# One inner block of a fused attention and MoE kernel by seven products instead of eight, with new order tables

## The chip, the core and the metric

The kernel runs on one core of a Trainium2 chip. The metric is the device time of one execution in microseconds (us); a median over several executions is quoted, and one profiled execution gives the trace that is read below. The engines are named as in the profile: PE is TensorE's matmul, PEld its weight load, DVE is VectorE, ACT is ScalarE, POOL is GpSimd, SP is SyncE, which issues nearly all transfers.

## What is computed

A linear attention with decay, then two feed-forward layers ("MoE layers" in the code). Cut to what matters:

```python
# attention: batch 2, 8 heads, 768 steps, head size 64
state = gamma * state + k_t (outer) v_t          # for t in range(768)
y_t   = scale * q_t @ state
x = y.transpose(0, 2, 1, 3).reshape(1536, 512)
# stage 1: w_in 512 x 2048, w_out 2048 x 512
h = x @ w_in
x = where(h > 0, h, exp(min(h, 0)) - 1) @ w_out
# stage 2: w_a, w_b 512 x 1536, w_out 1536 x 512
out = ((x @ w_a) * (x @ w_b)) @ w_out
```

## The kernel before

**Numbers.** Every fp32 operand of the layers is split into a high part that TensorE's fast fp32r form takes and a low rest: `wh`/`wl` for weights, `xh`/`xl` and `yh`/`yl` for the inputs of stage 1 and 2, `gh`/`gl` for what comes out of the first product of a stage. One product of 128 rows is then three matmuls (high by high, high by low, low by high). A split is a cast on ACT (L746) and a subtraction on POOL or DVE (L750). The weights come as 64-bit words into one of three staging buffers (`raw`); ACT takes their two halves apart (L768, L772) and DVE joins them (clamp L775, shift L779, join L783, total L789). So each weight tile costs DVE four instructions before its split.

**Attention.** `attention()` works on eight pairs of heads. `load` (L366 to L383) issues the transfers of q and k of a pair (one tensor `in_qk`) and of k and v by rows (`in_kv`). For pairs 0 to 3 q and k come in two pieces, `q0` (columns 0 to 511) and `q1` (columns 512 to 767); for the others in one. The order of the transfers is `QUEUE`, that of TensorE's steps `PRODUCTS`: `("s",u,part)` are scores (L556), `("x",p)` turns k of a pair (L483), `("t",u)` are states (L519), `("r",n,part)` results of two pairs (L584, L591), `("m",f,half)` the first four tiles of stage 1's first product for token block 0 (L709 to L711). `keep_warm` (L332) fills places in which the planner expects TensorE to wait. The score banks are two, so a score step waits until DVE has masked the one before the last (L562).

**Layers.** `layers()` has three blocks of 512 tokens (b = 0, 1, 2) and inner blocks of 128 (f). Two blocks and two weight tiles make a 2 by 2 product of quarter matrices, which `quad` does by seven products p1 to p7 of six matmuls each instead of eight; the sums that it needs of the inputs (`differences`, L1114 and on) and of the weights (`sums`, L816) are made on DVE and split again. Block 2 has the same within itself with 256 columns (`quad_s`), and `plain1`, `plain2` are the products without sums. `contract1` and `contract2` are the second products of stage 1 and stage 2 (L709 to L711).

In stage 2 inner block f has the tiles wa[f] and wb[f]. For f = 0 the kernel before uses `plain2` for all three blocks: four products of twelve matmuls for blocks 0 and 1, two for block 2, as undivided steps `R0.b.0` and `R0.b.1`. Block 1's plain product also has to be over before `differences` writes its third sum into that block's buffer (the argument `lambda: done["plain", 2, 1]`). From f = 1 on `quad2` does blocks 0 and 1.

**Order.** TensorE's order in the layers is the table `STEPS`: `a`, `d`, `b` are stage 1's first tiles (plain products of blocks 1 and 2, first second-product), `qf.i` and `rf.i` the products of `quad` and of block 2 in stage 1, `cn.b.e` stage 1's second products, and `Q`, `R`, `o` the same in stage 2. The other engines' order is made by the planner `Sched` from fixed costs and the times by which each step is wanted; on POOL or DVE, whichever suits (`other=("DVE", 0.6)`). All waits are set when the program is built.

Of the kernel before, what the change touches and what calls it, by code (L numbers as in the profile page):

```python
# [33 lines left out]
a2 a3 a4 a6 a0 d0 a5 b0 a1 a7 b1 d2 q4.2 d1 d3 b2 c0.1.3 q4.1 c0.1.1 c0.1.2 c0.1.0 q4.5 b3 c0.2.1 q4.6 r4.1 q4.3  # L34
r4.2 r4.6 c0.2.0 q4.7 r4.5 c0.2.2 r6.1 q6.1 r4.3 q4.4 c0.2.3 r4.7 r6.2 q6.6 q6.2 q6.5 c1.1.1 c1.0.1 c1.0.2 r6.6
r4.4 q6.7 c1.0.0 c1.0.3 c1.1.2 r6.7 q6.3 q6.4 c1.2.3 c1.2.2 r6.5 c1.1.0 c1.2.0 c1.1.3 r8.2 r6.3 r6.4 r8.1 q8.1
c2.1.2 c2.0.0 c2.0.1 r8.6 c2.1.0 q8.2 c2.1.3 q8.6 c2.1.1 r8.5 q8.7 r8.7 c1.2.1 c2.2.2 q8.5 c2.2.0 c2.2.3 q10.1
q8.4 q10.5 r8.4 r8.3 c2.0.2 q8.3 q10.2 q10.3 r10.2 c3.0.0 c2.2.1 q10.6 c2.0.3 c3.0.2 q10.7 c3.1.1 q12.1 r10.1
c3.0.3 r10.6 c3.2.1 r10.7 c3.1.2 q10.4 c3.0.1 c3.2.0 c3.2.2 q12.5 r12.1 r10.5 c3.2.3 r10.3 q12.2 r12.2 c3.1.0
c4.0.0 r12.5 r14.1 c3.1.3 c4.0.1 r10.4 r12.3 q12.6 c4.0.2 c4.1.3 q14.1 c4.2.3 r12.6 c4.1.0 q12.7 q14.5 c4.1.1  # L40
q14.2 q14.6 c4.0.3 q12.3 r12.7 c4.2.2 c4.2.0 r12.4 c4.2.1 q12.4 c4.1.2 q14.3 r14.6 c5.1.1 q14.7 c5.1.0 r14.7
c5.2.1 q14.4 c5.1.2 c5.1.3 c5.0.1 c5.2.3 c5.0.0 c5.0.3 r14.5 c5.0.2 c6.1.2 r14.4 c5.2.0 r14.2 r14.3 c6.1.3
c6.1.0 c5.2.2 c6.0.0 c6.1.1 c6.0.3 c6.2.2 c6.0.2 R0.1.0 c6.0.1 c6.2.0 c6.2.1 c6.2.3 R0.1.1 R0.0.0 R0.2.0 Q1.2
Q1.5 R2.2 Q1.1 R1.2 R1.0 R1.3 Q1.6 R0.2.1 Q1.3 R1.1 Q2.1 Q2.2 R0.0.1 Q1.7 Q2.6 R2.1 Q1.4 Q2.5 o0.8 o0.5 o0.3
o0.7 o0.10 Q2.3 o0.2 o0.11 Q3.1 Q2.7 R3.1 R2.5 R2.6 R3.2 Q2.4 R3.6 Q3.5 o0.9 Q3.2 Q3.6 R2.7 o0.4 o0.1 Q4.1 R4.1
R2.4 Q3.7 o0.6 o0.0 Q3.4 Q3.3 R3.7 R3.5 Q4.2 R4.2 R4.6 Q4.6 R3.4 R3.3 Q4.5 R2.3 Q4.7 o1.1 o1.2 Q4.3 Q5.1 o1.11
o1.0 R5.1 o1.9 Q5.2 o1.8 R4.5 o1.5 o1.4 R4.7 R5.2 Q4.4 o1.3 R4.4 Q6.1 R5.6 Q5.6 R5.5 R4.3 Q5.7 o1.7 R5.7 R5.3
Q5.5 R5.4 R6.5 o1.10 R6.2 o1.6 Q5.3 Q5.4 R6.1 Q6.5 R6.6 R6.3 o2.0 o2.7 o2.11 o2.6 Q6.3 Q6.6 o2.10 Q7.1 R6.7 R7.2
o2.3 R6.4 Q6.7 Q6.2 Q7.6 Q7.2 Q8.1 R7.1 o2.2 Q6.4 R7.6 Q7.5 R7.5 Q7.7 Q7.3 o2.4 R7.7 o2.5 R8.5 R7.3 o2.1 o2.9
Q8.6 R8.1 R8.2 R8.3 Q8.5 R7.4 Q7.4 o2.8 Q8.7 Q8.2 Q8.3 R8.6 o3.9 o3.7 o3.8 R9.2 Q10.1 o3.5 R8.7 o3.11 o3.2 Q8.4  # L50
R8.4 o3.0 o3.3 R9.1 Q9.2 Q9.1 R9.6 R9.5 Q9.6 R9.7 R9.3 o3.4 R10.1 Q10.6 R9.4 o3.1 o3.6 Q9.7 Q9.5 o3.10 Q10.2
Q9.3 Q11.2 Q10.5 R10.6 Q10.7 R10.2 Q10.3 Q9.4 o4.5 Q11.1 o4.10 R11.1 Q11.5 Q10.4 o4.0 o4.4 o4.1 R10.7 Q11.6 o4.6
Q11.7 o4.9 o4.3 o4.11 o4.2 R11.6 Q11.4 Q11.3 R11.7 o4.7 o4.8 R10.5 R11.5 o5.0 R11.3 o5.1 o5.2 o5.3 R11.2 R11.4
# [1396 lines left out]
```

## Time and profile before

| | us |
|---|---|
| three timed runs, median | 581.99 (581.75 to 582.2) |
| the profiled execution | 582.04 |
| its span in the trace | 580.3 |
| first step of the layers on TensorE | 60.28 after the span's start |
| TensorE busy, of the span | 574.5 |
| VectorE busy, of the span | 497.9 |

The span is 1.74 us shorter than the execution; the profiled execution lies 0.05 us from the median. A matmul's end is modelled in the trace, so TensorE's pace is read from the starts of its instructions, and a wait shows as a start that comes later than the pace. Times in the rows count from the span's start.

### The profile page before, as it was taken

The page shows a single profiled execution, that of the slowest core. Times are in us where ns is not written, and L with a number is a line of the kernel's source. Part 1 is how long each engine was busy: PE and PEld are TensorE (multiplying, and loading weights), DVE is VectorE, ACT ScalarE, POOL GpSimd, SP SyncE. Part 2 cuts the span into 40 slices and gives each one's busy share as a digit, 9 for nine tenths or more (in the row PEclk, how much of TensorE's full clock was granted, in tenths as well). Part 3 has the DMA queues.
Part 4 walks back from the last instruction along what each step waited for, and adds up shares of the span by engine and source line. Part 5 has one row for each costly group of instructions (what it writes and reads, how often), then busy time and mean ns, then how long its engine had stood idle before and what let it go on. Part 6 is the DMA issues. An engine that isn't in the chain of part 4 may idle for free.

```text
span 580.3 us, 9157 instructions
## 1 busy us (share of the span) xinstructions
PE 574.5 (99%) x3416; PEld 488.9 (84%) x3416; DVE 497.9 (86%) x816; ACT 346.1 (60%) x633; POOL 224.9 (39%) x165
## 2 busy tenths in 40 slices
PE   9999999999999999999999999999999999999997
PEld 8887888888888888888888888888888888888886
DVE  3886899988998999989998998989889998869565
ACT  6456897778577957687565675653554463454110
POOL 0355227415334334145477332252543174152210
PEclk9999999999999999999999999999999999999999
DMA  8993240122222223222210320313022231210013
GB/s 305 357 298 138 84 135 1 37 60 88 67 73 71 81 64 92 99 73 74 72 37 0 110 72 26 119 39 110 29 88 81 95 111 37 73 37 0 1 73 146
DMA packets 23421, 51.53 MB, mean 89 GB/s; under 512 B 2256, under 2 KB 11984, under 8 KB 23376
## 3 DMA queue, kind: packets, MB, share of 16 engines
q1 hardware_dynamic: 23232, 50.80, 28.1%
q8 instruction: 27, 0.44, 0.3%
q14 instruction: 18, 0.15, 0.1%
q10 hardware_dynamic: 144, 0.14, 0.1%
HBM read 47.79 MB, written 3.15 MB: 88 GB/s over the span
## 4 chain that ended last, share of the span: by engine, by line
PE 93%; DMA 5%; DVE 1%; issue 0%; SPq 0%; ACT 0%; DVEq 0%; ACTq 0%
PE p L848 49%; PE p L709 13%; PE p L710 13%; PE p L711 13%; DMA qk<-in_qk 2%; DMA raw<-in_w 1%; DMA rows<-in_kv 1%; PE y L591 1%; PE sc L556 1%; PE s L519 1%; PE y L584 1%; PE sc L483 0%; DVE wl L750 0%; ACT rows L498 0%; DVE a L779 0%
## 5 line engine op out<-in xcount | busy, mean ns | idle before, releaser
L750 POOL TENSOR_TENSOR wl<-a,wh 128x512 fp32r<-128x512 f32 x57 | 82.0, 1443 | 163.6 <-ACT wh L746 127.2
L750 POOL TENSOR_TENSOR gl<-t,gh 128x512 fp32r<-128x512 f32 x59 | 83.6, 1423 | 112.4 <-ACT gh L746 94.0
L746 ACT CAST wh<-a 128x512 fp32r<-128x512 f32 x98 | 59.6, 620 | 30.7 <-DVE a L789 19.1
L709 PE MATMUL p<-gh,wh 128*128 128x512 f32 x192 | 75.0, 390 | 0.0
L710 PE MATMUL p<-gl,wh 128*128 128x512 f32 x192 | 75.0, 390 | 0.0
L711 PE MATMUL p<-gh,wl 128*128 128x512 f32 x192 | 74.7, 389 | 0.0
L848 PE MATMUL p<-yl,wh 128*128 128x512 f32 (+1 forms) x200 | 69.5, 347 | 0.0
L848 PE MATMUL p<-yh,wh 128*128 128x512 f32 (+1 forms) x200 | 69.3, 347 | 0.0
L848 PE MATMUL p<-yh,wl 128*128 128x512 f32 (+1 forms) x200 | 69.3, 347 | 0.0
L848 PE MATMUL p<-wl,wh 128*128 128x256 f32 (+1 forms) x198 | 67.1, 339 | 0.0
L848 PE MATMUL p<-wh 128*128 128x256 f32 (+1 forms) x198 | 66.9, 338 | 0.0
L848 PE MATMUL p<-wh,wl 128*128 128x256 f32 (+1 forms) x198 | 66.9, 338 | 0.0
L746 ACT CAST gh<-t 128x512 fp32r<-128x512 f32 x80 | 48.3, 618 | 28.6 <-DVE t L1013 8.3
L864 ACT COPY t<-p 128x512 f32<-128x512 f32 x55 | 32.1, 584 | 43.6 <-PE p L848 43.0
L871 DVE TENSOR_TENSOR t<-p,t 128x512 f32<-128x512 f32 x66 | 45.2, 685 | 14.8 <-PE p L848 9.1
L709 PE MATMUL p<-wh,gh 128*128 128x512 f32 (+1 forms) x146 | 56.6, 388 | 0.0
L710 PE MATMUL p<-wl,gh 128*128 128x512 f32 (+1 forms) x146 | 56.6, 388 | 0.0
L711 PE MATMUL p<-wh,gl 128*128 128x512 f32 (+1 forms) x146 | 56.4, 386 | 0.0
L768 ACT ACTIVATE a<-raw 128x512 f32<-128x512 f32 x64 | 43.0, 673 | 17.3 <-POOL wl L750 8.1
L772 ACT ACTIVATE c<-raw 128x512 int32<-128x512 uint32 x64 | 42.8, 671 | 10.6 <-DVE a L789 9.5
L783 DVE SCALAR_TENSOR_TENSOR a<-raw,a 128x512 int32<-128x512 int32 x64 | 48.5, 768 | 0.5
L789 DVE CUSTOM_DVE_ANT_0 a<-a,c 128x1024 uint16<-128x1024 uint16 x64 | 47.5, 753 | 0.7
(142 smaller groups left out, 1346.7 us busy)
## 6 DMA issues: line engine op xcount, KB each, us to landing
raw<-in_w SPq DMA_DIRECT2D x16, 512.0 KB, 3.8
raw<-in_wa SPq DMA_DIRECT2D x12, 512.0 KB, 3.8
...
```

The lines of the kernel that those rows point to most:

```text
L709: nc.tensor.matmul(ps, lh, rh, start=first, stop=False)
L710: nc.tensor.matmul(ps, lh, rl, start=False, stop=False)
L711: nc.tensor.matmul(ps, ll, rh, start=False, stop=last)
L746: nc.scalar.copy(like(dst[key][0], src()), src())
L750: engine.tensor_tensor(out=lo, in0=src(), in1=hi.bitcast(F32), op=ALU.subtract)
L768: nc.scalar.activation(out=T["a", key], in_=T["raw", key][:, :, 1].bitcast(F32), func=AF.Abs, scale=E_SHIFT)
L772: nc.scalar.activation(out=T["c", key], in_=T["raw", key][:, :, 0].bitcast(U32), func=AF.Copy, scale=2.0**-29)
L783: nc.vector.scalar_tensor_tensor(out=ai, in0=T["raw", key][:, :, 1], scalar=SIGN, in1=ai, op0=ALU.bitwise_and, op1=ALU.bitwise_or)
L789: nc.vector.tensor_tensor(out=ai, in0=ai, in1=T["c", key], op=ALU.add)
L848: nc.tensor.matmul(ps, l[:, col(cc)], r, start=first and i + j == 0, stop=end and j == 2, skip_group_check=True)
L864: "ACT", 0.48, lambda ring: nc.scalar.copy(taken(key, ring), T[src]), after, [(tr, users)], [bank],
L871: "DVE", 0.6, lambda: nc.vector.tensor_tensor(out=T[out], in0=T[in0], in1=T[in1], op=op), after,
```

## The change

Five things are changed, and nothing of what is computed. (1) In stage 2, f = 0 goes through `sums` and `quad2` as the other inner blocks do; its plain products of blocks 0 and 1 are gone, block 2's stay, cut in two parts each (`R0.0` to `R0.3`). (2) `differences` of stage 2 waits for no plain product. (3) `STEPS` is a new order of all steps of both layers. (4) `QUEUE` and `PRODUCTS` are new orders for the attention, and q and k of pairs 0 to 3 come in one transfer each. (5) The planner's cost of an `x` step is 1.38 instead of 0.9. Two lines stand for each table:

```diff
 STEPS = """
-a2 a3 a4 a6 a0 d0 a5 b0 a1 a7 b1 d2 q4.2 d1 d3 b2 c0.1.3 q4.1 ...
+a2 a6 a3 d3 d0 d2 b0 r4.2 b1 a0 a4 b2 a5 a7 a1 b3 r4.1 d1 c0.1.0 ...
-c6.1.0 c5.2.2 c6.0.0 c6.1.1 c6.0.3 c6.2.2 c6.0.2 R0.1.0 c6.0.1 c6.2.0 ...
+c6.0.0 c6.1.1 c6.1.0 c6.0.1 c6.1.3 c6.2.0 c6.2.3 Q0.1 c6.2.1 Q1.1 c6.0.2 ...
 QUEUE = [
-    "tb", ("q0",1), ("q1",1), ("q0",0), ("q1",0), ("v",1), ("k",3), ("v",0), ("v",3), ("k",2), ("q0",3), "gy",
+    ("q",1), "tb", ("q",0), ("k",3), ("v",1), ("v",3), ("v",0), ("q",3), "gy", ("q",2), ("k",2), ("v",2),
 PRODUCTS = [
-    ("s",3,0), ("s",2,0), ("r",0,1), ("t",2), ("s",2,1), ("s",3,1), ("r",1,0), ("s",4,0), ("t",4), ("r",1,1),
+    ("s",3,0), ("s",2,0), ("r",0,1), ("t",2), ("s",3,1), ("s",2,1), ("r",1,0), ("s",5,0), ("s",4,0), ("r",1,1),
...
-            done["q0", 0] = load(0, "qk", 1.3, "q0", col=h0)
             t1_ = fetch("tb", 0.3, lambda: nc.scalar.dma_start(out=tb1, in_=tab[:, : NS1 + C]))
-            done["q1", 0] = load(0, "qk", 0.7, "q1", col=h1)
+            done["q0", 0] = done["q1", 0] = load(0, "qk", 1.95, "q")
...
-                if p in (0, 1, 2, 3) and p:
+                if p in () and p:
...
-                    o = step(("x", p), 0.9, turn, [done["q0", p], done["q1", p], eye_], [(rsc, t_)], [users["qk", p]])
+                    o = step(("x", p), 1.38, turn, [done["q0", p], done["q1", p], eye_], [(rsc, t_)], [users["qk", p]])
...
-        weight(("wa", 0)), weight(("wb", 0))
-        for f in range(1, NF2):
+        for f in range(NF2):
             sums(("wa", f), ("wb", f))
...
-        for b in (1, 0):
-            go(f"R0.{b}.", plain2(0, b, 1))
...
-            lambda: done["plain", 2, 1],
+            list,
...
-        go("R0.2.", plain2(0, 2, 1))
-        for f in range(1, NF2):
+        for f in range(NF2):
...
-            if f % 2 == 0:
+            if f and f % 2 == 0:
```

How the order of instructions moves at three places, in the rows of the built programs. (In the kernel after, line numbers from 390 on are one lower, and from about 1385 on up to five lower.)

SP's first transfers, of before. The names are the tile, then the tensor; the size is partitions by elements.

```order
L379 DMA qk<-in_qk 128x2x512
L379 DMA qk<-in_qk 128x2x256
L379 DMA qk<-in_qk 128x2x512
L379 DMA qk<-in_qk 128x2x256
L381 DMA rows<-in_kv 128x768
L381 DMA k<-in_kv 128x768
```

And of after:

```order
L379 DMA qk<-in_qk 128x1536 x2
L381 DMA k<-in_kv 128x768
L381 DMA rows<-in_kv 128x768
L381 DMA k<-in_kv 128x768
L381 DMA rows<-in_kv 128x768
L379 DMA qk<-in_qk 128x1536
```

The first score step, which waited for the 512 columns of pair 1, now waits for all its 768 of q and of k.

TensorE at the first use of a weight of stage 1's second group of tiles, w1[4], of before: the end of `d2` and the start of `q4.2`. `wh_1097` and `wl_1098` are w1[4].

```order
L848 MATMUL p_1127<-xh_676,wh_723 128x512
L848 MATMUL p_1127<-xl_677,wh_723 128x512
L848 MATMUL p_1127<-xh_676,wl_724 128x512
L848 MATMUL p_1159<-xh_343,wh_1097 128x512
L848 MATMUL p_1159<-xl_344,wh_1097 128x512
L848 MATMUL p_1159<-xh_343,wl_1098 128x512
```

And of after: the end of `b0` and the start of `r4.2`; w1[4] is `wh_1076` and `wl_1077`.

```order
L708 MATMUL p_1064<-gh_803,wh_987 128x512
L709 MATMUL p_1064<-gl_804,wh_987 128x512
L710 MATMUL p_1064<-gh_803,wl_988 128x512
L847 MATMUL p_1088<-xh_643,wh_1076 128x256
L847 MATMUL p_1088<-xl_644,wh_1076 128x256
L847 MATMUL p_1088<-xh_643,wl_1077 128x256
```

Ahead of it stand, in the layers, 96 matmuls before (`a2 a3 a4 a6 a0 d0 a5 b0 a1 a7 b1 d2`) and 66 after (`a2 a6 a3 d3 d0 d2 b0`).

VectorE's rows up to the low part of w1[4], of before (the 20th to the 27th of its instructions in the layers):

```order
L775 TENSOR_SCALAR a_1056<-a_1056 128x512
L889 SCALAR_TENSOR_TENSOR t_1052<-t_1052,p_943 128x512
L779 TENSOR_SCALAR a_1056<-a_1056 128x512
L783 SCALAR_TENSOR_TENSOR a_1056<-raw_1004,a_1056 128x512
L789 ISA a_1056<-a_1056,c_1064 128x1024
L750 TENSOR_TENSOR wl_1078<-a_986,wh_1077 128x512
L789 ISA a_1013<-a_1013,c_1061 128x1024
L750 TENSOR_TENSOR wl_1098<-a_1056,wh_1097 128x512
```

And of after (the 18th to the 24th):

```order
L774 TENSOR_SCALAR a_1041<-a_1041 128x512
L778 TENSOR_SCALAR a_1041<-a_1041 128x512
L782 SCALAR_TENSOR_TENSOR a_1041<-raw_983,a_1041 128x512
L788 ISA a_1041<-a_1041,c_1044 128x1024
L888 SCALAR_TENSOR_TENSOR t_1047<-t_1047,p_994 128x512
L778 TENSOR_SCALAR a_1011<-a_1011 128x512
L749 TENSOR_TENSOR wl_1077<-a_1041,wh_1076 128x512
```

VectorE has three instructions less ahead of it, TensorE thirty matmuls less.

TensorE where stage 2 begins, of before: the end of `c6.0.2` and the start of `R0.1.0`, twelve matmuls of which the first six stand here (`yh`, `yl` are stage 2's input, `wh_3131` is wa[0]).

```order
L711 MATMUL p_3365<-gh_3222,wl_3015 128x512
L848 MATMUL p_3375<-yh_3314,wh_3131 128x512
L848 MATMUL p_3375<-yl_3315,wh_3131 128x512
L848 MATMUL p_3375<-yh_3314,wl_3132 128x512
L848 MATMUL p_3375<-yh_3314,wh_3131 128x512
L848 MATMUL p_3375<-yl_3315,wh_3131 128x512
L848 MATMUL p_3375<-yh_3314,wl_3132 128x512
```

And of after: `c6.2.3`, then `Q0.1` with six matmuls, then `c6.2.1` (wa[0] is `wh_2996`).

```order
L710 MATMUL p_3381<-gh_3337,wl_2985 128x512
L847 MATMUL p_3391<-yh_3342,wh_2996 128x512
L847 MATMUL p_3391<-yl_3343,wh_2996 128x512
L847 MATMUL p_3391<-yh_3342,wl_2997 128x512
L847 MATMUL p_3391<-yh_3342,wh_2996 128x512
L847 MATMUL p_3391<-yl_3343,wh_2996 128x512
L847 MATMUL p_3391<-yh_3342,wl_2997 128x512
L708 MATMUL p_3406<-gh_3326,wh_2980 128x512
```

The step of twelve matmuls on block 1 has given way to one of six on block 0.

## Rows read from the trace of the kernel before

**Rows 1.** The page: busy time by engine, and the longest chain by engine.

```profile
PE 574.5 (99%) x3416; PEld 488.9 (84%) x3416; DVE 497.9 (86%) x816; ACT 346.1 (60%) x633; POOL 224.9 (39%) x165
...
PE 93%; DMA 5%; DVE 1%; issue 0%; SPq 0%; ACT 0%; DVEq 0%; ACTq 0%
```

**Rows 2.** The longest chain in order of time: start, us, what.

```profile
257.34 1.36 PE p L848 x6
```

**Rows 3.** Timeline of TensorE and VectorE near 232: start, us, instruction.

```profile
232.24 0.28 PE L848 MATMUL p<-xl,wh 128*128 128x256 f32 x1
232.62 0.39 PE L848 MATMUL p<-xh,wl 128*128 128x256 f32 x1
232.84 0.28 PE L848 MATMUL p<-xh,wh 128*128 128x256 f32 x1
232.96 0.28 PE L848 MATMUL p<-xl,wh 128*128 128x256 f32 x1
...
230.78 1.78 DVE L750 TENSOR_TENSOR wl<-a,wh 128x512 fp32r<-128x512 f32 x1
```

**Rows 4.** Timeline of TensorE in the attention; in brackets idle time and its releaser.

```profile
5.62 1.16 PE L556 MATMUL sc<-qk 64*128 64x128 f32 x16 [0.36 <-DMA qk<-in_qk]
...
8.00 0.94 PE L332 MATMUL warm<-kv 128*128 128x128 f32 x6
8.87 1.55 PE L483 MATMUL sc<-one,qk 64*128 64x64 f32 x24
...
21.36 0.80 PE L519 MATMUL s<-rows 128*64 128x64 f32 x20
22.11 0.71 PE L556 MATMUL sc<-qk 64*128 64x128 f32 x8
23.24 0.71 PE L556 MATMUL sc<-qk 64*128 64x128 f32 x8 [0.41 <-DMA qk<-in_qk]
23.88 0.96 PE L584 MATMUL y<-qk,st 64*64 64x128 f32 x24
...
46.19 0.33 PE L519 MATMUL s<-rows 128*64 128x64 f32 x2 [0.40 <-ACT rows L498]
...
47.42 0.51 PE L584 MATMUL y<-qk,st 64*64 64x128 f32 x8
...
60.28 0.50 PE L848 MATMUL p<-xh,wh 128*128 128x512 f32 x1
```

**Rows 5.** First piece of the longest chain; then busy times, clock, DMA share, GB/s.

```profile
0.73 4.85 DMA qk<-in_qk
...
8.00:12.00 4.00, 4.00 (x68) 3.72 (x66) 0.99 (x2) 4.00 (x12) 0.00 (x0) 1.00 1.04 407
```

**Rows 6.** Timelines of VectorE, GpSimd and TensorE where the layers begin.

```profile
62.42 0.56 DVE L775 TENSOR_SCALAR a<-a 128x512 f32<-128x512 f32 x1 [1.25 <-ACT a L768]
63.01 1.40 DVE L779 TENSOR_SCALAR a<-a 128x512 int32<-128x512 int32 x1
...
66.71 0.43 DVE L779 TENSOR_SCALAR a<-a 128x512 int32<-128x512 int32 x1
...
77.97 0.68 DVE L750 TENSOR_TENSOR wl<-a,wh 128x512 fp32r<-128x512 f32 x1
...
61.40 2.73 POOL L636 TENSOR_TENSOR xl<-yf,xh 128x512 fp32r<-128x512 f32 x2
...
82.62 0.39 PE L848 MATMUL p<-xh,wl 128*128 128x512 f32 x1
```

**Rows 7.** The page's costliest groups: count, busy us, mean ns of one, idle before.

```profile
L750 POOL TENSOR_TENSOR wl<-a,wh 128x512 fp32r<-128x512 f32 x57 | 82.0, 1443 | 163.6 <-ACT wh L746 127.2
...
L746 ACT CAST wh<-a 128x512 fp32r<-128x512 f32 x98 | 59.6, 620 | 30.7 <-DVE a L789 19.1
...
L871 DVE TENSOR_TENSOR t<-p,t 128x512 f32<-128x512 f32 x66 | 45.2, 685 | 14.8 <-PE p L848 9.1
```

**Rows 8.** Busy us in two stretches: PE, PEld, DVE, ACT, POOL; clock, DMA share, GB/s.

```profile
270.00:300.00 30.00, 30.00 (x145) 25.30 (x144) 28.02 (x49) 18.80 (x34) 16.31 (x12) 1.00 0.22 67
300.00:330.00 30.00, 30.00 (x137) 24.95 (x136) 26.11 (x35) 16.98 (x30) 18.69 (x12) 1.00 0.21 61
```

More of the change, by code (lines that the diff above doesn't have):

```diff
@@ L33 @@
 STEPS = """
[L34 to L53, printed above, removed]
@@ L54 @@
-R10.4 R10.3 o5.4 o5.5 o5.6 o5.7 o5.8 o5.9 o5.10 o5.11 o5.12
+a2 a6 a3 d3 d0 d2 b0 r4.2 b1 a0 a4 b2 a5 a7 a1 b3 r4.1 d1 c0.1.0 c0.1.1 c0.1.2 r4.5 c0.1.3 q4.5 r4.3 q4.1 c0.2.3
+c0.2.0 r4.6 r6.1 c0.2.1 q4.6 r4.7 q4.3 c0.2.2 q4.7 r6.2 r4.4 q6.1 r6.6 r6.5 q4.2 q6.5 r6.7 q4.4 c1.2.0 c1.1.3
+q6.6 r6.3 c1.2.1 c1.1.0 q6.3 c1.1.1 q6.7 r8.2 q8.1 c1.1.2 c1.0.2 c1.2.3 q8.6 c1.0.1 q6.4 q6.2 r6.4 q8.5 c1.2.2
+c1.0.0 q8.7 c2.1.2 c1.0.3 q8.2 r8.5 q8.4 r10.1 c2.0.1 c2.1.1 c2.1.3 r8.1 q10.2 c2.1.0 r8.6 c2.2.1 c2.0.0 c2.2.0
@@ new lines @@
+r8.7 q8.3 q10.1 r10.6 c2.2.2 r10.5 r8.4 c2.0.3 r8.3 c2.0.2 q10.6 c2.2.3 q10.5 c3.0.0 c3.1.2 r10.3 q10.7 r12.2
+r10.2 q12.2 q10.3 c3.2.0 r10.7 c3.0.2 q12.1 r10.4 c3.0.1 c3.0.3 c3.1.1 r12.1 c3.1.0 q10.4 c4.1.2 q14.1 c3.1.3
+c3.2.3 c3.2.1 c3.2.2 c4.0.3 c4.1.0 c4.1.3 c4.0.1 q12.5 q14.5 r12.5 c4.1.1 r12.6 r12.3 q12.6 q12.3 q12.7 c4.0.2
+c4.2.2 c4.2.1 q14.2 q14.6 q12.4 c4.2.0 r12.7 c4.2.3 c4.0.0 r14.1 r12.4 r14.5 q14.3 c5.1.2 c5.1.0 q14.7 r14.6
+c5.0.0 c5.2.0 q14.4 c5.1.3 c5.0.1 c5.1.1 c5.2.1 r14.7 c5.0.3 r14.2 c5.2.3 c5.0.2 c6.1.2 r14.3 r14.4 c5.2.2
@@ new lines @@
+c6.0.0 c6.1.1 c6.1.0 c6.0.1 c6.1.3 c6.2.0 c6.2.3 Q0.1 c6.2.1 Q1.1 c6.0.2 c6.2.2 R1.2 R0.0 c6.0.3 R0.2 Q0.6 R1.3
+R1.0 Q0.2 R1.1 Q0.7 Q1.2 Q0.5 Q1.5 R0.1 R0.3 Q1.6 R2.2 Q2.1 R2.1 Q2.5 Q1.3 Q0.3 Q1.7 o0.11 o0.8 Q2.2 Q0.4 o0.9
+Q1.4 o0.10 R3.1 o0.7 Q2.6 o0.3 Q2.3 Q2.7 o0.4 R3.2 Q3.1 Q2.4 o0.5 o0.6 R2.6 o0.1 R3.5 Q3.5 R3.3 Q3.6 o0.2 R2.7
+o0.0 R3.6 R2.5 Q3.3 Q3.7 R3.7 Q4.1 Q3.2 Q3.4 R4.1 R2.4 R4.2 R2.3 Q4.6 R4.5 R3.4 Q4.2 R4.6 Q4.5 o1.1 R4.3 o1.3
+Q5.2 R4.7 R5.2 o1.11 Q5.1 o1.9 R5.1 R4.4 Q4.7 Q4.3 o1.4 o1.10 Q4.4 R6.2 o1.8 Q5.6 R6.1 o1.2 R5.6 o1.0 o1.5 Q5.7
@@ new lines @@
+Q5.5 R5.5 o1.6 R5.7 Q5.3 R6.6 o1.7 Q6.5 Q6.2 R5.3 R5.4 R6.7 R6.5 Q5.4 o2.6 Q6.1 o2.5 R6.4 Q6.6 R7.2 o2.7 R6.3
+Q7.1 o2.10 Q6.7 o2.9 Q7.6 Q7.5 Q6.4 R7.1 Q7.2 Q7.3 Q7.7 R7.6 o2.3 R7.5 Q8.1 Q6.3 R7.7 o2.4 o2.2 o2.0 R8.5 R8.2
+Q7.4 R7.3 Q8.2 R7.4 Q8.5 R8.3 R8.1 o2.1 Q8.6 o2.8 o2.11 R9.1 Q8.7 Q9.2 o3.3 Q8.4 Q8.3 R8.6 o3.5 o3.4 o3.0 R8.7
+R9.5 R9.2 o3.6 o3.1 o3.2 Q9.5 o3.9 o3.10 Q9.1 o3.8 o3.7 R10.2 R9.6 Q9.6 Q9.3 Q9.7 o3.11 R10.1 Q10.1 R9.3 R10.6
+R9.7 R8.4 Q9.4 R9.4 R10.5 Q10.2 Q10.5 Q10.6 o4.11 o4.9 o4.5 o4.1 o4.6 o4.7 R10.7 o4.4 Q11.1 R10.3 Q10.3 Q10.7
@@ L55 @@
+Q11.2 o4.2 Q11.6 o4.8 Q11.5 R11.1 Q11.7 Q10.4 o4.10 Q11.4 R11.5 R11.6 o4.3 R11.3 o5.0 R11.7 Q11.3 o5.1 R10.4
+o5.2 R11.2 o5.3 R11.4 o5.4 o5.5 o4.0 o5.6 o5.7 o5.8 o5.9 o5.10 o5.11 o5.12
 """
 QUEUE = [
[3 rows of a table removed]
[3 rows of a table added]
 ]
 PRODUCTS = [
[5 rows of a table removed]
[5 rows of a table added]
 ]
@@ L388, in attention @@
             h0, h1 = slice(0, 4 * C), slice(4 * C, S)
-            done["q0", 0] = load(0, "qk", 1.3, "q0", col=h0)
             t1_ = fetch("tb", 0.3, lambda: nc.scalar.dma_start(out=tb1, in_=tab[:, : NS1 + C]))
-            done["q1", 0] = load(0, "qk", 0.7, "q1", col=h1)
+            done["q0", 0] = done["q1", 0] = load(0, "qk", 1.95, "q")
             eye_ = add("DVE", 0.35, unit_matrix, [t1_])
             for p in range(NPAIR):
-                if p in (0, 1, 2, 3) and p:
-                    done["q0", p] = load(p, "qk", 1.3, "q0", col=h0)
-                    done["q1", p] = load(p, "qk", 0.7, "q1", col=h1)
+                if p in () and p:
+                    done["q0", p] = load(p, "qk", 1.31, "q0", col=h0)
+                    done["q1", p] = load(p, "qk", 0.71, "q1", col=h1)
                 elif p:
```

12 rows, old and new, of tables (PRODUCTS, QUEUE) are left out of this document.

## The prediction

> **What bounds the kernel now.** The page first: TensorE is busy for 99% of the span, VectorE for 86%, and the longest chain lies on PE for 93% [rows 1]. The reader should see that VectorE has little in hand, though it does not bind. A busy PE need not be at its peak, so the second view is the chain in order of time: in the layers six matmuls of 512 columns take 1.36 us, 0.227 each [rows 2], whole stretches long. The third is TensorE's timeline, in which I looked for starts later than that pace. From 60.28 us, where the layers begin [rows 4], to the end I found one: near 232 two starts of 256-column matmuls follow the last by 0.38 and 0.22 us, where the next distance is 0.12 [rows 3]. So 0.26 + 0.10 = 0.36 us are lost there, behind a VectorE subtraction that runs from 230.78 to 232.56. All other loss is in the attention. The layers are thus bound by TensorE's count of matmuls, the attention in part by data and by other engines.
>
> **The change part by part.** The sum is made against the profiled execution: 580.3 us of span and 1.74 outside it, 582.04, which is 0.05 above the median of 581.99.
>
> *Seven products for f = 0.* Four products of twelve matmuls become seven of six: 48 become 42. Six matmuls go, 6 x 0.227 = **-1.36 us** [rows 2]. All lie on the path, since TensorE has no gap there. The helpers get more: two casts on ScalarE and one copy, two subtractions on GpSimd, some seven additions and products on VectorE. At most 7 x 0.685 = 4.8 us on VectorE, and 1.44 each on GpSimd [rows 7]. The cover is VectorE's idle time just before, 30.00 - 28.02 = 1.98 us and 30.00 - 26.11 = 3.89 us in two stretches of 30 [rows 8]: 5.9 against 4.8. I cost this at nothing. Without that cover the price is up to 4.8 us. The handover itself: `Q0.1` stands three products, 3 x 1.36 = 4.08 us, behind the last second product of its input; eviction, cast and subtraction take 0.685 + 0.62 + 1.44 = 2.75 us [rows 7], so the input is ready 1.3 us early.
>
> *The argument `list`* only takes away a wait on products that no longer exist: nothing.
>
> *The stall near 232* hangs on a place in the old order, and in the new one that weight has another: **-0.36 us** [rows 3].
>
> *The attention.* The old order has three places where TensorE lost time [rows 4]. A score step of eight matmuls starts at 22.11, the next at 23.24, 1.13 later and behind a transfer; the following distance is 0.64, so 0.49 is lost. Before 46.19 it idles for 0.40 behind ScalarE. The step at 46.19 holds TensorE for 1.23 us until 47.42, where one of ten times as many matmuls took 22.11 - 21.36 = 0.75, so 0.48 more is lost. Together **-1.37 us**, if the new order avoids all three. The bounds: 0 if they return elsewhere, -1.6 if the other short waits of the attention shrink as well. I take the measured sum, since one of the three hangs on a transfer that the whole loads finish earlier.
>
> *Whole loads.* This is what they cost. The first score step waits for q and k of its pair. Today that is 128 x 2 x 512 numbers, 524 thousand bytes, and 665 with the table (141) that comes beside it; it took 4.85 us from 0.73. At 407 GB/s [rows 5] 665 need 1.63 us, which leaves 3.22 fixed. The whole load has 786, with the table 927: 2.28 + 3.22 = 5.50, so it lands at 6.23 instead of 5.58. The price lies between 0 (there are other waits just behind, which may absorb it: TensorE fills 0.87 us from 8.00 with warm matmuls) and +0.65. I take **+0.45 us**, nearer to the full price, because the first step starts as its transfer lands, at 5.62 [rows 4]. The cost 1.38 for an `x` step only moves things: the 24 small matmuls span 8.87 to 10.4 either way. It counts with the order.
>
> *The new order in the layers.* All steps move, so I looked for the step with the least slack. It is `r4.2`, the first to use w1[4]. TensorE reaches its third matmul after 66 matmuls and two short ones: 66 x 0.227 + 0.24 = 15.2 us behind the layers' start. VectorE needs 23 instructions before the low part of that weight. In the kernel before that subtraction is the 27th and starts at 77.97; the first starts at 62.42, 2.14 us after the layers' start [rows 6]. So 26 took 15.55 us, 0.598 each. Then 23 x 0.598 = 13.75, the subtraction starts at 2.14 + 13.75 = 15.9 and ends 0.68 later, at 16.6: TensorE waits **+1.4 us**. In the old order there was slack: the part was done at 78.65 and first used at 82.62 [rows 6]. The bounds: +0.4, if the first shift takes 0.43 as the next one does, not 1.40 [rows 6], and +2.0 if one instruction more or a late staging buffer comes between. I take the middle, which is what the measured pace gives. Behind the waiting matmul all of TensorE's later steps are queued and come later by the same; VectorE, which then gets its next products to evict later, has that time to catch up.
>
> That slow shift deserves a look. At 63.01 it took 1.40 us while a GpSimd pair ran from 61.40 to 64.13; at 66.71, with GpSimd quiet, 0.43 [rows 6]. The Trainium skill, page "SBUF — State Buffer", section "🔬 SBUF: two separate sides", says that VectorE and GpSimd share a port pair that one of them holds for its whole instruction while the other is blocked. The two durations agree with it. By that rule the delay stays as long as that pair stays there, which speaks for the 1.4; without the block it would be 0.4.
>
> *Other waits of the new order.* Some hundred steps move, and the trace before does not show what they meet. Between 0 and 1.2 us (three stalls of the size of that near 232, rounded up); below nothing is excluded, since TensorE has no other gap to lose. I take **+0.2**, nearest to that one stall [rows 3].
>
> The sum: 580.3 - 1.36 - 0.36 - 1.37 + 0.45 + 1.4 + 0.2 = 579.26; with 1.74, **581.0 us**.
>
> **The rivals.**
>
> *B, the helpers keep up.* No wait at `r4.2`, since the planner has put ahead only what VectorE can do and the slow shift is gone: 581.0 - 1.4 - 0.1 = 579.5. For it: 0.97 of the 1.4 us is one shift [rows 6]. Against it: the count of 23 instructions at the measured pace.
>
> *C, VectorE becomes the bound.* Where the new order takes a weight earlier and VectorE's pace is slower than 0.65 us an instruction instead of 0.598, its backlog reaches two more weights in the first 70 us of the layers, each worth what `r4.2` costs: 581.0 + 2 x 1.4 = 583.8, slower than before. For it: 86% busy [rows 1], 28.02 of 30 us in a stretch [rows 8], and the added work. Against it: TensorE did not wait for it before, but near 232. The Trainium skill, page "Perfetto Trace Analysis", section "Identifying the Most-Contended Engine", says that TensorE is to be judged by its weight-load busy time and the others by occupancy. By these, 84% and 86% [rows 1], VectorE would be the bound already, and up to 4.8 us of added work would then show in the time. The evenly spaced starts of TensorE speak against it.
>
> *D, the attention gives nothing.* The first step starts later, the three stalls come back at other places; -1.37 and +0.45 cancel or leave the price: 581.9 to 582.4, say 582.1. For it: the attention's steps hang on transfers, whose total of bytes is unchanged. Against it: two of the three stalls have to do with order, not with bytes.
>
> *That the change doesn't do what it says*, I rule out for the matmuls: the order of the built program has six of them where twelve stood.
>
> **How the numbers follow.** About 0.2%, 1.16 us, is what a measurement of this kernel can tell from no change; so faster is below 580.8 and slower above 583.2. My forecast, 581.0, has 0.44: it lies close to the first bound, 0.17 of it on the faster side and 0.27 on the other. B has 0.27, all faster. D has 0.16, all within. C has 0.13, all slower. Faster 0.17 + 0.27 = 0.44, same 0.27 + 0.16 = 0.43, slower 0.13. The range: down to 578.9, which is B with the attention's larger gain (-1.6) and the whole loads at a smaller price; up to 582.9, which takes in D and the forecast with `r4.2` at 2.0 and the other waits at 1.2 (581.0 + 0.6 + 1.0 = 582.6). Left out are C and the lower tail of B, less than 2 in 10.
>
> **What would show it.** Each step can be read in the trace of the kernel after. TensorE's first score step starts near 6.1 (right) or 5.6 (then the whole load cost nothing). The first matmul of the layers starts near 59.4; at 60.3 or later, D holds. In `r4.2` a wait for VectorE's L749 near 74.5 us of more than 1 us, or none (B). Further starts of TensorE late by over 0.5 us between 75 and 130, behind VectorE, mean C. Six matmuls fewer in TensorE's count from the seven products, and no wait ahead of `Q0.1` and the following `Q` steps; a wait there would mean that the cover for the added helper work was too thin. The tail behind the last matmul should be as before. The prediction is wrong as a whole if TensorE's distance between 512-column matmuls is no longer 0.227, or if a stretch that I did not look at has become the longest chain.

## The result: slower by 0.5%, outside the range

| | us |
|---|---|
| after, six timed runs, median | 585.42 (584.04 to 586.16) |
| before, six runs beside it | 581.91 |
| ratio | 1.0053, 95% interval 1.0039 to 1.0067 |
| profiled execution after, its span | 586.13, 584.3 |

The forecast was 581.0 with a range up to 582.9. The change is slower by 3.5 us, which is more than the 0.2% that a measurement of this kernel can tell. Two lines of the page of after answer to [rows 1]: busy times, and the longest chain by engine.

```profile
PE 575.9 (99%) x3412; PEld 489.4 (84%) x3412; DVE 496.1 (85%) x824; ACT 345.5 (59%) x636; POOL 229.5 (39%) x166
...
PE 86%; DVE 6%; issue 4%; DMA 1%; ACT 1%; SPq 1%; POOL 0%; DVEq 0%; ACTq 0%
```

The busy shares hardly move, and a reader of these alone would not see that anything happened. (TensorE's count falls by four: 26 warm matmuls instead of 24, and six fewer in the layers.) The chain does move: 6% of it now lie on VectorE, where it was 1%. Where the time went is seen from TensorE's starts. In before the layers began at 60.28 [rows 4], and TensorE lost 0.36 us in them. The view of waits of after, TensorE in the layers (us in total, times, longest us), and its timeline at these places:

```profile
PE p L708 <- DVE xs L1209: 0.7, 1, 0.7
PE p L847 <- DVE t L888: 0.4, 1, 0.4
PE p L847 <- ACT t L863: 0.4, 1, 0.4
PE p L847 <- DVE wl L749: 0.4, 1, 0.4
PE p L709 <- DVE gl L749: 0.3, 1, 0.3
PE p L847 <- ACT wh L745: 0.2, 1, 0.2
```

```profile
61.93 0.50 PE L847 MATMUL p<-xh,wh 128*128 128x512 f32 x1
...
77.44 0.39 PE L847 MATMUL p<-xh,wh 128*128 128x256 f32 x1 [0.21 <-ACT wh L745]
77.67 0.28 PE L847 MATMUL p<-xl,wh 128*128 128x256 f32 x1
78.33 0.39 PE L847 MATMUL p<-xh,wl 128*128 128x256 f32 x1 [0.38 <-DVE wl L749]
...
95.17 0.50 PE L847 MATMUL p<-xh,wh 128*128 128x512 f32 x1 [0.40 <-DVE t L888]
...
98.67 0.50 PE L709 MATMUL p<-gl,wh 128*128 128x512 f32 x1 [0.26 <-DVE gl L749]
...
238.39 0.50 PE L708 MATMUL p<-gh,wh 128*128 128x512 f32 x1 [0.68 <-DVE xs L1209]
...
249.46 0.50 PE L847 MATMUL p<-xh,wh 128*128 128x512 f32 x1 [0.40 <-ACT t L863]
```

The idle times in brackets are less than what is lost, since the ends of matmuls are modelled. Measured by starts against the pace, as in the prediction, the five places cost 1.12 (r4.2, at 77 and 78), 0.67, 0.53, 0.95 and 0.67 us, together 3.95 with the slower start behind each. The account against the span of before: 580.3 + 1.65 (layers begin later) + 3.95 - 0.35 (the place near 232 is gone) - 1.36 (six matmuls) = 584.2, measured 584.3.

In the attention, TensorE's timeline (idle time and its releaser in brackets), then busy us of four stretches (PE, PEld, DVE, ACT, POOL; clock, DMA share, GB/s), then SP's issues:

```profile
5.62 1.88 PE L555 MATMUL sc<-qk 64*128 64x128 f32 x16
7.34 1.45 PE L482 MATMUL sc<-one,qk 64*128 64x64 f32 x24
...
30.58 1.16 PE L555 MATMUL sc<-qk 64*128 64x128 f32 x16
33.60 0.80 PE L518 MATMUL s<-rows 128*64 128x64 f32 x20 [1.86 <-DMA rows<-in_kv]
34.33 0.69 PE L708 MATMUL p<-xh,wh 128*128 128x512 f32 x1
34.81 0.63 PE L709 MATMUL p<-xl,wh 128*128 128x512 f32 x1
35.24 0.63 PE L710 MATMUL p<-xh,wl 128*128 128x512 f32 x1
```

```profile
20.00:24.00 4.00, 4.00 (x93) 3.69 (x92) 3.85 (x7) 2.17 (x5) 3.06 (x3) 1.00 0.72 254
24.00:28.00 4.00, 4.00 (x76) 3.67 (x68) 3.79 (x7) 0.67 (x2) 0.76 (x2) 1.00 0.87 314
...
32.00:36.00 4.00, 2.40 (x24) 2.08 (x25) 2.02 (x4) 2.17 (x5) 2.23 (x3) 0.81 1.08 290
36.00:40.00 4.00, 4.00 (x63) 3.13 (x63) 3.80 (x7) 2.43 (x5) 1.27 (x1) 0.76 1.02 405
```

```profile
13.14 7.90 SPq L379 DMA_DIRECT2D qk<-in_qk  x2
```

The first two stretches in before:

```profile
20.00:24.00 4.00, 3.56 (x68) 2.88 (x64) 3.23 (x7) 1.86 (x4) 2.18 (x3) 1.00 1.05 390
24.00:28.00 4.00, 4.00 (x80) 3.59 (x82) 3.79 (x7) 1.92 (x4) 0.21 (x1) 1.00 1.03 407
```

The three losses of [rows 4] are gone, and one of 1.86 us has taken their place. It waits for the rows of pair 4. SP stood from 13.5 to 20.7 at q of pair 4, which has no buffer until a result step of an earlier pair is over (SP's two issues of q fill 13.14 to 21.04 in one group), with the k and v of pairs 4 and 5 behind it; meanwhile the transfers ran dry, 254 and 314 GB/s where before had 390 and 407. Behind the wait TensorE's clock was granted at 0.81 and 0.76 of full speed in the next two stretches: between 1.2 and 2.4 GHz, so part of each at the lower level. Matmuls of 512 columns then follow each other by 0.43 us, not 0.23. Kernel e2 below has the same attention and a wait at the same step, but a clock of 1.00 behind it: from that step to the layers it takes 60.09 - 33.20 = 26.89 us, and after takes 61.93 - 33.60 = 28.33. So the clock cost 1.44 us here.

### The profile page after: what moved, and what is told of

It reads as the page before. It is cut to its first block, busy times and chain, and to the rows that moved or that the text cites. A ratio compares the mean times of both kernels' runs of the same rounds, so it can differ in the third digit from the quotient of the medians.

```text
span 584.3 us, 9177 instructions
## 1 busy us (share of the span) xinstructions
PE 575.9 (99%) x3412; PEld 489.4 (84%) x3412; DVE 496.1 (85%) x824; ACT 345.5 (59%) x636; POOL 229.5 (39%) x166
## 4 chain that ended last, share of the span: by engine, by line
PE 86%; DVE 6%; issue 4%; DMA 1%; ACT 1%; SPq 1%; POOL 0%; DVEq 0%; ACTq 0%
PE p L847 44%; PE p L708 12%; PE p L709 12%; PE p L710 12%; PE sc L555 2%; PE y L590 2%; DMA rows<-in_kv 1%; DVE a L815 1%; PE warm L332 1%; DVE xs L1209 1%; PE y L583 1%; PE s L518 1%; DVE wl L749 1%; DVE t L888 1%; DVE a L788 0%
## 5 line engine op out<-in xcount | busy, mean ns | idle before, releaser
L749 POOL TENSOR_TENSOR wl<-a,wh 128x512 fp32r<-128x512 f32 x59 | 86.5, 1470 | 183.1 <-ACT wh L745 146.3
L749 POOL TENSOR_TENSOR gl<-t,gh 128x512 fp32r<-128x512 f32 x59 | 84.0, 1430 | 102.2 <-ACT gh L745 68.7
L847 PE MATMUL p<-wl,wh 128*128 128x256 f32 (+1 forms) x204 | 69.3, 340 | 0.0
L847 PE MATMUL p<-wh 128*128 128x256 f32 (+1 forms) x204 | 69.2, 339 | 0.0
L847 PE MATMUL p<-wh,wl 128*128 128x256 f32 (+1 forms) x204 | 69.2, 339 | 0.0
L847 PE MATMUL p<-yl,wh 128*128 128x512 f32 (+1 forms) x192 | 66.4, 346 | 0.0
L847 PE MATMUL p<-yh,wh 128*128 128x512 f32 (+1 forms) x192 | 66.3, 345 | 0.0
L847 PE MATMUL p<-yh,wl 128*128 128x512 f32 (+1 forms) x192 | 66.2, 345 | 0.0
L782 DVE SCALAR_TENSOR_TENSOR a<-raw,a 128x512 int32<-128x512 int32 x64 | 46.9, 746 | 0.6
L788 DVE CUSTOM_DVE_ANT_0 a<-a,c 128x1024 uint16<-128x1024 uint16 x64 | 45.8, 730 | 1.1
L847 PE MATMUL p<-xh,wh 128*128 128x512 f32 (+1 forms) x128 | 45.2, 353 | 1.0 <-DVE t L888 0.4
```

Of the source, the lines that this page charges most:

```text
L749: engine.tensor_tensor(out=lo, in0=src(), in1=hi.bitcast(F32), op=ALU.subtract)
L782: nc.vector.scalar_tensor_tensor(out=ai, in0=T["raw", key][:, :, 1], scalar=SIGN, in1=ai, op0=ALU.bitwise_and, op1=ALU.bitwise_or)
L788: nc.vector.tensor_tensor(out=ai, in0=ai, in1=T["c", key], op=ALU.add)
L847: nc.tensor.matmul(ps, l[:, col(cc)], r, start=first and i + j == 0, stop=end and j == 2, skip_group_check=True)
```

## The experiments

Sixteen kernels; each is compared with runs of the kernel before on the same chip, 582.1 to 582.4 us. Late starts are summed as above. Kernels that mix the two orders use names of steps as in the section on the change.

**Which part costs: attention or layers.**

e1_old_attention:
```diff
 # kernel after, with these of before: QUEUE, PRODUCTS, loads of q and k, cost of x
-    ("q",1), "tb", ("q",0), ("k",3), ...
+    "tb", ("q0",1), ("q1",1), ("q0",0), ...
```


> The kernel after with the attention of before (its order of transfers, its halves of q and k, its order of products). Theory T: the attention of after loses time by itself, 1.65 us at the first matmul of the layers (61.93 against 60.28), and the new order of the layers by itself, 3.95 us of late TensorE starts in six places against 0.35 before and six matmuls less (1.36). Then the layers' waits stay as they are in after and the span is 580.3 - 1.36 - 0.35 + 3.95 = 582.5, the time 584.3. Rival R: the waits at 77 to 99 us (2.3 us of the 3.95) exist only because the attention of after hands VectorE over late; then they vanish here and the time is near 582.0.

Measured 585.14, ratio 1.0055 (1.0034 to 1.0075). The five places are all there, 1.17, 0.67, 0.53, 2.09 and 0.82 us: 5.28 in sum. So R falls, and T holds for the layers: they lose by themselves, and more than the 3.95 us of after. T's other half, that the attention of after loses 1.65 us, is not borne out: e1 is only 0.28 us below after in the median, and its layers begin at 61.15. In the twelve profiled kernels with the attention of before they begin anywhere from 59.75 (e6) to 61.18 (e8).

e2_new_attention is the reverse, the kernel before with the attention of after.

> The kernel before with the attention of after; the layers' order and plain products stay. T: only the attention's loss, span 580.3 + 1.65 = 581.95, time 583.7 where TensorE's clock falls as in the profile of after, and 2.0 less, 581.7, where it does not. R: the late hand-over makes VectorE late here too, so that TensorE waits in the first 40 us of the layers by 1 us or more, 584.7 or above.

Measured 582.04, ratio 1.0006 (0.9983 to 1.0029), and in the layers only the old place near 232 is late. The layers began at 60.09. The profiled run had a wait at the same step too, 2.10 us before 33.20 (the view puts it down to ScalarE, not to the transfer), but a clock of 1.00 behind it. Of its ten runs seven had a mean clock of 1.000 (581.1 to 582.4) and three 0.993 to 0.997 (584.6 to 586.0); in more than 60 runs of the kernel before none was under 0.999. So the new attention is worth next to nothing, and those three runs, with the lower clock, took some 2.5 to 4 us more.

**The attention's wait.**

e3_v4_first:
```diff
-("k",4), ("w",0), ("v",4), ("w",3)
+("k",4), ("v",4), ("w",0), ("w",3)
```


> The kernel after, one exchange in the order of transfers: v of pair 4 goes ahead of the weight tile w0, which nothing uses before 40 us. T: TensorE's wait of 1.86 us at 31.7 to 33.6 was for this transfer alone and the clock of 0.76 to 0.81 behind it (34 to 40 us) came from that wait; both go, the layers start at 61.93 - 1.9 - 2.0 = 58.0 and the time is 586.1 - 3.9 = 582.2 in each run. Rival: the wait goes to the next transfer (w0 comes later by 1.5 us and its products wait), then less than 1.9 us is won.

Measured 586.39, ratio 1.0077 (1.0049 to 1.0105): a miss, the rival's way. TensorE in the attention, waits:

```profile
PE y L583 <- DVE st L526: 1.9, 1, 1.9
```

The state step now starts at 31.30 without a wait. But ScalarE and VectorE take w0 in their order, wait for its later transfer, and the state scan that TensorE needs stands behind that: 1.9 us again. The clock fell again as well, to 0.60 between 36 and 40 us.

e5_kv5_first:
```diff
-("q",5), ("q",4), ("k",5), ("v",5), ("k",4)
+("q",5), ("k",5), ("v",5), ("q",4), ("k",4)
```


> The kernel after, one exchange in the order of transfers: k and v of pair 5 go ahead of q of pair 4, which has to wait for a buffer until 20.7 us and holds everything behind it. Theory T: TensorE's wait at 31.7 to 33.6 comes from transfers that run dry there (254 and 314 GB/s from 20 to 28 us against 390 and 407 in the kernel before, some 0.9 MB or 2.3 us less); with 0.8 MB issued ahead of the blocked load the rate stays near 400, the wait is gone, the clock stays at 1.00 in 32 to 40 us and the layers start at 58.0 to 58.5 instead of 61.9; time 585.4 - 2.7 = 582.7 (2.7: the 1.9 of the wait and, in about half of the runs, 2.0 of clock). Rival: the order of the transfers does not matter since the sum of bytes sets the time, as the exchange of v4 and w0 left the time where it was; then 585.4 again, with the wait at another place.

Measured 585.7, ratio 1.0064 (1.004 to 1.0087). The stretch of 20 to 24 us of this kernel, and TensorE's waits in its attention:

```profile
20.00:24.00 4.00, 4.00 (x82) 3.61 (x78) 3.85 (x7) 1.95 (x5) 2.80 (x3) 1.00 1.03 400
```

```profile
PE s L518 <- DMA rows<-in_kv: 1.1, 1, 1.1
...
PE sc L555 <- DMA qk<-in_qk: 0.6, 1, 0.6
PE p L710 <- POOL wl L454: 0.2, 1, 0.2
```

The first half of the theory holds, 400 GB/s where there were 254; the second does not. The 1.9 us come back as 1.1 + 0.6 + 0.2, and the layers begin at 61.4. The dry stretch is not what limits the attention; filled or not, two microseconds are waited for. That the sum of bytes is the limit fits all three attentions, but no run with fewer bytes was made, so it is not shown.

e4_busy_wait:
```diff
+                    for _ in range(6 * (u == 4)):
+                        nc.tensor.matmul(ps[:, :C], zero, zero, start=True, stop=True)
```


> The kernel after with six more warm matmuls (some 1.7 us) ahead of the state step of pair 4, in the place of TensorE's wait at 31.7 to 33.6; nothing else changes. T: the transfer still sets the start of that step (33.6), but the clock stays at 1.00 from 32 to 40 us, so the layers start at 61.93 - 2.0 = 59.9 and each run takes 584.1 instead of 584.0 to 586.2. Rival: the lower clock has nothing to do with the idle time; then the runs still spread over 2 us and the layers start at 61.9 in some.

Measured 585.58, ratio 1.0065 (1.0039 to 1.009). In the profile the state step starts at 33.75, the clock is 1.00 and the layers begin at 60.66, 1.27 us earlier than in after. Five of six runs had a clock of 1.000, one 0.997. But the times still spread, 584.0 to 588.6, probably for a reason in the layers (last section). The clock's part is seen in the trace, not in the median: inconclusive.

**The layers: one step moved, and less work for VectorE.**

e8_later_r42:
```diff
-a2 a6 a3 d3 d0 d2 b0 r4.2 b1 a0 a4 b2 ...
+a2 a6 a3 d3 d0 d2 b0 a0 a4 r4.2 b1 b2 ...
```


> The kernel e1_old_attention with r4.2 two steps later and b1 behind it (b0 a0 a4 r4.2 b1 instead of b0 r4.2 b1 a0 a4), so that w1[4] is wanted 2.7 us later. If the late places are a matter of local order: 1.1 us are won, 585.1 - 1.1 = 584.0, and the other places (94, 98, 238, 250 us) stay as they are. If VectorE's throughput is the bound over the first 40 us of the layers: the wait vanishes at r4.2 and the places at 94 and 98 us grow by as much, 585.1 again.

Measured 585.41, ratio 1.0056 (1.0039 to 1.0073). TensorE's timeline:

```profile
92.36 0.39 PE L847 MATMUL p<-xh,wh 128*128 128x256 f32 x1 [0.16 <-DVE t L888]
...
94.78 0.50 PE L847 MATMUL p<-xh,wh 128*128 128x512 f32 x1 [1.44 <-DVE t L888]
```

The 1.17 us at `r4.2` are gone and come back 16 us later: up to 99 us the late starts sum to 2.71, where they were 2.37. A wait that moves with its sum kept speaks for helpers that are behind, and not for one step placed too early. The engine that comes last at these places is VectorE. It is not VectorE's work alone, though. In after VectorE has hardly any idle time from 64.00 to 84.73; then it idles twice itself, behind GpSimd and behind ScalarE, which in turn had waited for VectorE. Two pieces of the longest chain of after, in order of time, and two rows of VectorE's timeline:

```profile
65.80 18.52 issue
84.31 1.58 POOL wl L749
```

```profile
85.92 1.80 DVE L815 TENSOR_TENSOR a<-a 128x256 f32<-128x256 f32 x4 [1.19 <-POOL wl L749]
...
92.00 0.69 DVE L888 SCALAR_TENSOR_TENSOR t<-t,p 128x512 f32<-128x512 f32 x1 [1.12 <-ACT t L893]
```

The first piece (issue is time in which an engine waits for nothing that the profile shows) is GpSimd's, and points at a remedy that was not tried: it did nothing for 18.5 us, while VectorE did five subtractions of the same kind (L749) for weights between 69.92 and 82.24. Whether moving them would gain is open, since the two engines slow each other (last section).

Three kernels leave out VectorE's last instruction for a weight tile, the addition of its low bits, so their weights are coarser. The instructions that are left keep their order on every engine (in e9 against e1: 698 of VectorE, 571 of ScalarE, 142 of GpSimd), so nothing but VectorE's work changes.
```diff
             def total():
-                ai = T["a", key].bitcast(I32)
-                nc.vector.tensor_tensor(out=ai, in0=ai, in1=T["c", key], op=ALU.add)
+                pass
```


> e1_old_attention (the new layers, the old attention), with VectorE's last step of a weight tile left out in the layers (the addition of the low bits, L789, 0.6 us each, 74 of them; the weights are coarser by it). The order of all else stays. Theory V: all late starts of TensorE in the layers come from VectorE, which has no idle time to give in stage 1; with some 5 us less to do in the first 40 us and 0.6 for each later weight, every one of the five places is gone: 585.1 - 4.5 = 580.6. Rival: the places come from chains through ScalarE, GpSimd or transfers, or from the banks; then at least those at 94 us (a bank) and 250 us (ScalarE) stay, 583 to 584.

> The kernel before with the same addition left out. V: TensorE waited for VectorE at one place only, so 582.1 - 0.36 = 581.7. The difference to e9_new_order_less_dve is what the seven products are worth when VectorE does not bind, 1.36 less what the attention's spread adds: 1.0 to 1.4.

e9 took 583.26, ratio 1.0013 (0.9996 to 1.003), e10 582.09, ratio 0.9988 (0.9975 to 1.0001). The busy line of e9's page, and TensorE's waits in its layers:

```profile
PE 574.7 (99%) x3410; PEld 488.0 (84%) x3410; DVE 458.0 (79%) x760; ACT 344.3 (59%) x636; POOL 223.0 (38%) x166
```

```profile
PE p L847 <- ACT t L863: 0.5, 1, 0.5
PE p L710 <- DVE gl L750: 0.2, 1, 0.2
```

With 39 us less VectorE work the late starts fall from 5.28 to 2.15 us, and the median by 1.9 (the profiled run of e1 was the slowest of its four; profile against profile the span falls by 3.3). The same relief gives before only its one place, 0.36 us in the trace, within the noise of the time. So VectorE's work is the cause of most of it, 3.1 of 5.3 us, and not of all: 0.77 us at 246.6 stay behind a copy on ScalarE (in after ScalarE had itself waited 1.18 us for VectorE just ahead of that copy), and e9 stays slower than e10, so theory V is right in direction, and its size, 4.5 us, was more than twice what came.

**The seven products.** e12_plain_f0 has the attention and stage 2 of before, with stage 1 in the order of after.

> The reverse mixture: attention of before, stage 1 in the order of after, stage 2 with plain products and in the order of before (the hand-over as in before). V: the waits of stage 1 come from its order, not from the seven products: the same five places, so e1_old_attention plus the six matmuls, 585.1 + 1.4 = 586.5, and no wait in stage 2, since VectorE has its lead there. Rival: the seven products' added helper work is what makes VectorE late in stage 1 (its sums are made there ahead of time); then the places at 238 and 250 us shrink and the time is 583.5 to 585.

Measured 587.81, ratio 1.0098 (1.0064 to 1.0132). The late places are the same five, 5.56 us, and none lies in stage 2. Between the profiled runs the spans differ by 586.4 - 584.9 = 1.5 from e1; less 0.28 of late starts and plus 0.09 of a later beginning of the layers in e1, 1.3 are left for six matmuls. The medians differ by 2.7 with wide spreads. So the seven products bring about what was worked out, and the five late places come with stage 1's order, whichever stage 2 follows.

**Mixtures of the orders.** e6_old_stage1 joins before's stage 1 to after's stage 2; e11_mixed_less_dve is the same with the addition left out.

```diff
 # steps of after
-a2 a6 a3 d3 ... (stage 1 of after) c6.0.0 c6.1.1 ... Q0.1 ...
+a2 a3 a4 a6 ... (stage 1 of before) c6.0.0 c6.1.1 ... Q0.1 ...
```


> The attention and stage 1 in the order of before, up to the last second-products of stage 1; from there the order of after, f = 0 by seven products. T: all that the layers lose comes from the new order of stage 1 (five late places between 77 and 250 us), and the seven products bring their 1.36 us: 582.0 - 1.36 = 580.7, no late start of TensorE in the layers but the one near 232. Rival: stage 2 gained nothing either, the old order meets waits at the hand-over, or VectorE is late there because of the helpers' added work: 582 or more.

> e6_old_stage1 (old stage 1, new stage 2) with the same addition left out. V: the waits at 308 to 338 us (5.6 us) are VectorE's too, which in that mixture comes to stage 2 with no lead; they go, 582.1 - 1.36 - 0.3 = 580.4, as e9. Rival: they are in the hand-over itself (the plain products that covered it are gone, sums and splits of GpSimd and ScalarE come late); then 584 or more.

e6 took 586.69, ratio 1.0079 (1.0051 to 1.0106). Stage 1 has no late place but the one near 232, and stage 2 has 5.6 us of them between 308 and 339, of which two:

```profile
321.00 0.50 PE L847 MATMUL p<-wh 128*128 128x512 f32 x1 [1.19 <-ACT wh L745]
...
322.65 0.50 PE L847 MATMUL p<-wh,wl 128*128 128x512 f32 x1 [0.91 <-DVE wl L749]
```

e11 took 584.82, ratio 1.0042 (1.0027 to 1.0057), with 3.4 us of them left, behind ScalarE's cast and GpSimd. That after itself has no late place there may be because its helpers come ahead while TensorE waits in stage 1; this is not shown, since the order of the helpers differs too: between 270 and 345 us only 62 of after's 103 VectorE instructions stand in e6 in the same order.

e7_both has e6's layers and e5's attention.

> The order of the layers of e6_old_stage1 with the attention of e5_kv5_first (whole loads, k and v of pair 5 ahead of q of pair 4). T: both gains add, 582.0 - 1.36 - (60.3 - 58.3 = 2.0) = 578.6. Rival: with the attention 2 us shorter VectorE starts the layers with less lead, and the first weights come late as in after: 579.5 to 580.5 with waits near 75 us.

Measured 587.3, ratio 1.009 (1.0061 to 1.0119); neither gain is there to be added.

Four more kernels were to tell local waits from a shortage. All have the attention of before.

```diff
 # e13: the first 147 steps of before, then after's     e14: the first 36 of before, then after's
 # e15, steps of after:
-c4.1.3 c4.0.1 q12.5 q14.5 r12.5 ... q12.6 q12.3 q12.7 c4.0.2
+c4.1.3 q12.5 q14.5 r12.5 c4.0.1 ... q12.6 q12.3 c4.0.2 q12.7
 # e16: e14 and e15 together
```


> The attention and the first 147 steps of the layers in the order of before, all later ones in the order of after (both orders hold the same 147 steps up to there, near 265 us), f = 0 by seven products. If the waits of e6_old_stage1 at 308 to 338 us came from where the two orders were joined, at the hand-over: they go, and with no late place in the first 265 us the time is 582.1 - 1.36 - 0.1 = 580.7. If the new stage 2 needs the lead that the helpers got from TensorE's waits in stage 1: they stay, 585 or more.

> The layers of after with only their first 36 steps in the order of before (the same 36). If the waits at 77, 94 and 98 us (2.4 us) are due to the order of these steps: they go, 585.1 - 2.4 = 582.7, with those at 238 and 250 us left. If VectorE's throughput is short whatever the order: they come later, between 100 and 240 us, 585.1.

> The layers of after with two steps moved: c4.0.1 three steps later (its place waits at 238 us for VectorE to free a bank) and q12.7 one step later (it waits at 250 us for ScalarE's copy of q12.6, two steps ahead). If both are local: 0.95 to 2.1 and 0.7 us are won, 585.1 - 2.2 = 582.9. If VectorE's backlog near 238 us is the cause, the next step that needs a bank or a weight waits instead, and only the 0.7 of q12.7 is won, 584.4.

> e14_old_first_36 and e15_two_later together, with the attention of before. If all three edits hold: no late place is left but small ones, 582.1 - 1.36 - 0.2 = 580.5, faster than both kernels. If waits only move: 583 to 585.

Measured: e13 587.52 (ratio 1.0099, 1.0082 to 1.0116), e14 589.57 (1.0131, 1.0109 to 1.0154), e15 592.29 (1.019, 1.0147 to 1.0234), e16 593.85 (1.02, 1.0181 to 1.022). Every hope of a gain failed. In e13 the waits at 308 to 339 stay. In e14 those before 100 us vanish and 3.3 us come back at 129 to 135. In e15 a product that needs a weight part waits in place of the moved step; TensorE's timeline and the stretch around it:

```profile
240.67 0.80 PE L847 MATMUL p<-wh,wl 128*128 128x512 f32 x1 [2.24 <-DVE wl L749]
241.26 0.63 PE L847 MATMUL p<-wh 128*128 128x512 f32 x1
```

```profile
240.00:244.00 4.00, 3.33 (x11) 2.95 (x12) 3.15 (x8) 1.28 (x2) 0.00 (x0) 0.57 0.15 15
```

Behind the 2.24 us the clock is down to 0.57, and 4.8 us of new waits follow at 315 to 345. In none of these kernels did moving a step remove its wait without others coming up. One thing these four cannot separate: the planner orders the helpers' work anew by the times at which TensorE's steps want it, so an edited table also changes VectorE's, ScalarE's and GpSimd's order. Between 270 and 345 us 57 of after's 103 VectorE instructions keep their order in e15, although its edit is near 240. (In e8 this matters little: 752 of the 762 in the layers stand as in e1.) How much of these new waits is shortage and how much a worse order of the helpers stays open. No version was found that beats the kernel before.

## Why the prediction was wrong, step by step

- **Bound by TensorE's count of matmuls.** Right for the kernel before, but taken too far. [rows 8] showed VectorE busy for 28.02 of 30 us, and the prediction used its idle time only as cover for the added helper work. A new order is a new schedule of demands on VectorE as well.
- **Seven products, -1.36.** Right: 1.3 by e1 and e12, six matmuls fewer in the layers, and no wait ahead of `Q0.1` or the steps behind it in after. The cover held there. In e6 and e13, with stage 1 or most of it as before, it did not; whether in after it came from TensorE's own waits in stage 1 stays open.
- **The stall near 232, -0.36.** Right, gone.
- **The attention, -1.37 in the hope that the losses do not return.** Wrong. Rival D, at 0.16, described it: the three come back as one. e2 gives 0 (-0.06 in the median). One reading behind the 1.37 was wrong without changing it: the step at 46.19 has 20 matmuls like the one it was compared with, two in the row shown and 18 from 46.70 on. What neither the forecast nor D had is the clock: the profiled run began its layers 1.65 us later, 1.44 of it for the lower clock behind that wait. In the runs of after it comes to 1.7 us (585.97 to 586.16 at a mean clock of 0.997, 584.04 to 584.88 at 1.000).
- **Whole loads, +0.45.** Wrong by its whole size: the first score step starts at 5.62 as in before, and at 5.37 in e2. The slow first steps of after (5.62 to 7.34) are not due to them either: in e1, with the old loads, the same steps lasted from 5.56 to 7.10. In both, pairs of these matmuls follow each other by 0.21 us at first and by 0.11 later, as at the two levels of the clock; the trace's record of the granted clock begins only at 7.17 and 6.73 us, where the distance changes. What the prediction did not look for is in the order of the loads: one that waits for its buffer holds all behind it (SP from 13.5 to 20.7). Filling that gap (e5) gave nothing, so even this is not shown to be the limit.
- **`r4.2`, +1.4.** Right in place, cause and nearly in size: 1.12 in after, 1.17 in e1. VectorE's first instruction came 2.07 us behind the layers' start (2.14 estimated) and the subtraction for w1[4] started 13.59 later (13.75). The slow shift was there too, 1.41 us at 64.67. The rest of the difference is TensorE itself, which was held before that by the high part.
- **Other waits of the new order, +0.2 within 0 to 1.2.** This is the term that failed most. It measured 2.8 us in the profile of after and 4.1 in e1. In that profile the 5.0 us by which the span exceeds the forecast are 2.6 from here and 2.6 from the attention with its loads (+1.65 where -0.92 was forecast), less 0.3 at `r4.2`; over all runs, where the attention comes to about nothing, this term is much the larger. The bound was made from the size of the one stall of before; but that stall belonged to an order which fitted VectorE, and says nothing on one that does not. The step with the least slack was looked for and found, and the search stopped there. The prediction let VectorE catch up while TensorE waits at `r4.2`; instead TensorE waited for it again 17 and 20 us later, and e8 shows that these waits do not hang on that one. The tell-tale that the prediction named for rival C, late starts of over 0.5 us between 75 and 130 behind VectorE, is what the trace has at 95.17 and 98.67. C had 0.13 and 583.8; its mechanism was the right one, its places too few. Its condition, a pace slower than 0.65 us an instruction, did not come true: 13.59 us for the first 23 instructions are 0.591. VectorE was not slower, it was asked for more sooner.
